# Pooled attention and a maxout feed-forward on one core: keys turned by the DMA crossbar, stores of whole tiles, one more half group, and first adds of batch 0's values on VectorE

## The chip, the cores and the metric

The kernel runs on one core of one Trainium2 chip. The metric is the device time in microseconds (us) of one execution. Before the change it is 242.86 us, the median of 3 runs (242.78 to 244.19). A core has five engines with queues of their own, which run in parallel and wait for each other by semaphores: TensorE (PE in the profile) for matmuls and transposes, VectorE (DVE), ScalarE (ACT), GpSimd (POOL), and SyncE (SP), which here only issues DMAs. Results of TensorE land in PSUM; DVE and ACT copy them to SBUF, the working memory. DMAs move data between SBUF and the memory in which inputs and outputs lie; a DMA can also transpose 16-bit data on its way through the crossbar.

## The reference, cut to what matters

There are 8 batches, 8 heads, 576 rows and 64 columns per head. Keys and values are averaged over groups of 8 rows, so that 72 pooled rows remain; each query attends to these. The attention output goes through three weight matrices of 512 x 768, of whose products the elementwise maximum is taken, and then through one of 768 x 512:

```python
k_p = k.reshape(B, H, Sp, pool, D).mean(axis=3)
v_p = v.reshape(B, H, Sp, pool, D).mean(axis=3)
scores = scale * np.matmul(q, k_p.transpose(0, 1, 3, 2))
...
x = np.ascontiguousarray(attn_out.transpose(0, 2, 1, 3)).reshape(B * S, H * D)
h = np.maximum(np.maximum(x @ w1, x @ w2), x @ w3)
return (h @ w_out)
```

## The kernel before

**Tokens and blocks.** The 4608 tokens are worked in 9 blocks of 512, numbered 0 to 8. Block n runs `hidden` (for each of 6 column groups jc of the hidden layer, three weight matrices, so 18 steps called slots) and then `project` (4 tiles of 128 tokens, one slot each). Attention of batch b = n + 1 is laid between the slots of block n, since a batch of 576 tokens is needed from block n + 1 on. Nothing is left to a scheduler: the order in which the code emits instructions is the order in which each engine runs them, and the plan (a table from slot to steps) says after which slot which step is emitted. Steps are named by a letter: `k` fills the key tile, `s` does the scores and exponentials of a head, `v` the attention values of 128 tokens, `x` their transposition into xT, `T` the transposition of the next batch's queries by DMA.

**Keys.** POOL folds the keys of batches 2 to 7 by adds into kps, twice side by side (`fold_k`, line 144, called from `pool_work`). `keys` (L171) turns kps on TensorE in six transposes into a PSUM tile pkt, and `fill_kz` (L177) copies it in two halves into kz, the layout that the scores need; batch 1 uses ACT for these copies and the others DVE (L187). Batch 0 is done ahead of block 0 by hand.

**Values of batch 0.** `pool_v` (L152) sums the 8 rows of each group on TensorE: 8 matmuls against an identity matrix, accumulating in PSUM, then a DVE copy to vp_all. It is called for heads 0 to 3, 4 to 5 and 6 to 7 (lines 418 to 421), in between the scores of the second half of the tokens (`scores2`). The other batches' values are folded on POOL.

**Start of block 0.** Block 0 begins when only the first 128 tokens are through attention. `hidden` therefore splits its work by columns of tokens (lines 315 and 316): group 0 for tokens 0 to 127 and 128 to 255, group 1 for tokens 0 to 255, then groups 0 and 1 for tokens 256 to 511, and the remaining groups in full width. `plan` of block 0 (lines 447 to 453) lays the rest of batch 0's attention and all of batch 1's between these slots.

**Stores.** A tile of 128 rows in osb holds two groups of 64 tokens: the tokens of a batch are kept in the order of their remainder g by 9, in the sequence GS. Row r of group g belongs to output row 9 r + GS[g]. Each group is stored by a DMA of its own (lines 337 to 341), 64 rows of 2 KB, issued by SP. The last tile is projected in two column halves, which ACT and DVE copy; there SP and ACT issue one group each. osb has 5 buffers, so a store has until the fifth next tile.

**SP's queue** holds, in order of emission, the query transposes, the xT transposes of batches 2 and later (`turn_x`, L220) and the stores. An entry that waits holds up those behind it.

Of the kernel before, what the change touches and what calls it, by code (L numbers as in the profile page):

```python
# [10 lines left out]
ALU = mybir.AluOpType  # L11
# [3 lines left out]
def kernel(  # L15
# [11 lines left out]
    nc = tc.nc  # L27
    dt = mybir.dt
    F32, BF16, F16 = dt.float32, dt.bfloat16, dt.float16

    B, H, S, D = q.shape
    POOL = 8
    Sp = S // POOL
# [8 lines left out]
    NG = 9  # L42
    GS = (0, 2, 4, 6, 8, 1, 3, 5, 7)
    NR = 64
    KCH = C // 128
    JCH = DFF // 128
    TOK = B * S
    NB = 512
    PSUM = bass.MemoryType.PSUM

    const = ctx.enter_context(tc.tile_pool(name="const", bufs=1))
    ld = ctx.enter_context(tc.tile_pool(name="ld", bufs=2))
    sb2 = ctx.enter_context(tc.tile_pool(name="sb2", bufs=2))
# [1 line left out]
    psp = ctx.enter_context(tc.tile_pool(name="psp", bufs=1, space=PSUM))  # L55
    ctx.enter_context(tc.manual_schedule())

    kts, vts, qbs, kps, qTs, ets = {}, {}, {}, {}, {}, {}

    def after(loads, first):  # L60
        for x in loads:
# [47 lines left out]
    identh = const.tile([128, 128], F16, name="identh", tag="identh")  # L109
    make_identity(nc, identh)  # L110
    for i in range(3):
# [6 lines left out]
        out=wo_sb, in_=moe_w_out.rearrange("(jc p) c -> p jc c", p=128))  # L118
# [22 lines left out]
    def new_kp(b):  # L141
        kps[b] = sb2.tile([96, 6, 2, D], BF16, name="kp", tag="kp")
# [9 lines left out]
    def pool_v(b, h, g, tag, evac):  # L152

        pvp = psp.tile([128, g - h, D], F32, name="pvp", tag=tag[0], bufs=tag[1])
        for j in range(POOL):
            nc.tensor.matmul(pvp, identh[0:Sp, :], vts[b][:, h:g, j, :],  # L156
                             start=(j == 0), stop=(j == POOL - 1))
        evac(out=vp_all[:, b, h:g, 0:D], in_=pvp[0:Sp])

    def turn_q(b, n0, n1, evac, tag):  # L160
# [10 lines left out]
    def keys(b, tag):  # L171
        pkt = psp.tile([128, 6, 96], BF16, name="pkt", tag=tag[0], bufs=tag[1])
        for i in range(6):
            nc.tensor.transpose(pkt[:, i, :], kps[b][:, i, :, :], ident[0:96, 0:96])  # L174
        return pkt

    def fill_kz(b, par, h0, h1, pkt, evac):  # L177
        rows = slice(64 * par, 64 * par + 64)
        evac(out=kz_all[b % 2][rows, par, h0:h1, 0:Sp].rearrange(  # L179
                 "p h (r i) -> p h r i", i=6),  # L180
             in_=pkt[rows, :, 12 * h0:12 * h1].rearrange("p i (h r) -> p h r i", r=12))

    def turn_k(b):
        pkt = keys(b, TR)
        for par in range(2):
            fill_kz(b, par, 0, H, pkt,
                    nc.scalar.copy if b == 1 else nc.vector.tensor_copy)  # L187

    def pool_k(b, tag):

# [61 lines left out]
    TR = ("tr", 1)  # L252
# [5 lines left out]
    def do(b, steps):  # L258

        for name in steps.split():
            i = int(name[1:] or 0)
            if name[0] in "qQ":
                turn_q(b, *QS[i], nc.vector.tensor_copy if name[0] == "Q"
                       else nc.scalar.copy, TR)
            elif name[0] == "T":
                qTs[b] = sb2.tile([128, 2 * NG, 128], BF16, name="qT", tag="qT")
                nc.sync.dma_start_transpose(  # L270
                    out=qTs[b], in_=qbs[b].rearrange("p hp t d -> p (hp t d)"))
            elif name[0] == "k":
                turn_k(b)
            elif name[0] == "K":
                pool_k(b, PW)
            elif name[0] == "a":
                nc.vector.tensor_tensor(out=k16, in0=kts[b][:, :, 0:4],
                                        in1=kts[b][:, :, 4:8], op=ALU.add)
            elif name[0] == "s":
                if i == 0:  # L280
                    new_et(b)
                scores(b, i)
            elif name[0] == "v":
                xns[b, i] = values(b, CHUNKS[i][0])
            else:
                turn_x(b, *CHUNKS[i], xns[b, i], TR,
                       nc.vector.tensor_copy if name[0] == "X" else nc.scalar.copy)
# [23 lines left out]
    def hidden(n, hT):  # L311

        parts = [(0, JCH, 0, NB)]
        if n == 0:
            parts = [(0, 1, 0, 128), (0, 1, 128, 256), (1, 2, 0, 256), (0, 2, 256, NB),
                     (2, JCH, 0, NB)]
        elif n == 1:
            parts = [(0, 1, 0, 256), (0, 1, 256, NB), (1, JCH, 0, NB)]
        for j0, j1, c0, c1 in parts:
            for jc in range(j0, j1):  # L320
                yield from hidden_part(n, jc, c0, c1, hT)

    def project(n, hT):
        for mm in range(4):
            m = 4 * n + mm
            last = m == TOK // 128 - 1
            osb = sb3.tile([128, C], F32, name="osb", tag="osb", bufs=5)
            for c in ((slice(0, C // 2), slice(C // 2, C)) if last else (slice(0, C),)):
                po = psp.tile([128, c.stop - c.start], F32, name="po", tag="pw", bufs=3)
                for jc in range(JCH):  # L330
                    nc.tensor.matmul(po, hT[:, jc, bass.ts(mm, 128)], wo_sb[:, jc, c],  # L331
                                     start=(jc == 0), stop=(jc == JCH - 1))
                if c.start:
                    nc.vector.tensor_copy(out=osb[:, c], in_=po)
                else:
                    nc.scalar.copy(out=osb[:, c], in_=po)  # L336
                for u in range(2):
                    b, g = divmod(2 * m + u, NG)
                    dst = out[S * b:S * b + S, :].rearrange("(r g) c -> r g c", g=NG)
                    (nc.scalar if last and u else nc.sync).dma_start(  # L340
                        out=dst[:, GS[g], c], in_=osb[64 * u:64 * u + 64, c])
            yield

    def new_hT():
# [8 lines left out]

    new_et(0)
    ATT = ("att", 2)
    new_kp(0)
    k16 = const.tile([96, 6, 4, D], F16, name="k16", tag="k16")
    heat(17)
    for i in range(0, 6, 2):
        src = kts[0][:, i:i + 2] if i else kt0  # L360
        f = const.tile([96, 2, 4, D], F32, name="kf", tag="kf")
        nc.vector.tensor_tensor(out=f, in0=src[:, :, 0:4], in1=src[:, :, 4:8],  # L362
                                op=ALU.add)
        nc.vector.tensor_tensor(out=f[:, :, 0:2], in0=f[:, :, 0:2], in1=f[:, :, 2:4],  # L364
                                op=ALU.add)
        nc.vector.tensor_tensor(  # L366
            out=kps[0][:, i:i + 2].rearrange("p i a d -> p a i d"),
            in0=f[:, None, :, 0].to_broadcast([96, 2, 2, D]),
            in1=f[:, None, :, 1].to_broadcast([96, 2, 2, D]), op=ALU.add)
    turn_q(0, 0, 5, nc.vector.tensor_copy, PW)  # L370
    turn_q(0, 5, 9, nc.scalar.copy, ATT)
    pkt0 = [keys(0, PW) for _ in range(2)]
# [4 lines left out]
    def scores4(h):  # L377
        psc = psp.tile([128, 4, 256], F32, name="psc4", tag="att", bufs=2)
        for i in range(4):
            score(0, h + i, psc[:, i, :], 0, 0, 4)  # L380
        exp(ets[0][:, h:h + 4, 0:256], psc[0:Sp])

    def scores2(h):
        psc = psp.tile([128, 2, 512], F32, name="psc2", tag="att", bufs=2)
        for i in range(2):
            score(0, h + i, psc[:, i, 0:64], 0, 4, 5)
            score(0, h + i, psc[:, i, 64:320], 1, 0, 4)
        exp(ets[0][:, h:h + 2, 256:S], psc[0:Sp, :, 0:320])
# [26 lines left out]
    turn_q(0, 14, 18, nc.vector.tensor_copy, PW)  # L415
    heat(2)
    scores4(4)
    pool_v(0, 0, 4, PW, nc.vector.tensor_copy)
    scores2(0)
    pool_v(0, 4, 6, PW, nc.vector.tensor_copy)  # L420
    pool_v(0, 6, 8, PW, nc.vector.tensor_copy)
    scores2(2)
# [9 lines left out]
    def block(n, plan):  # L432

        hT = new_hT()
        slot = 0
        for part in (hidden(n, hT), project(n, hT)):
            for _ in part:
                if slot == 0 and n > 0:
                    pool_work(n, mms[-1])
                for b, steps in plan.get(slot, ()):  # L440
                    if b < B:
                        do(b, steps)
                slot += 1

    fold_v(1)
    fold_k(2, nc.gpsimd)
    block(0, {0: [(0, "X1")], 3: [(0, "v2")], 5: [(0, "v3")], 6: [(0, "x2")],
              8: [(0, "x3")], 10: [(0, "v4")], 12: [(0, "x4")],
              13: [(1, "a")], 15: [(1, "K")], 17: [(1, "k")], 19: [(1, "Q0")],
              20: [(1, "Q1")], 21: [(1, "Q2 s0")], 22: [(1, "Q3 s1")],  # L450
              23: [(1, "s2 s3")], 24: [(1, "s4 s5")], 25: [(1, "s6 s7")],
              26: [(1, "v0")], 27: [(1, "v1 x0"), (2, "T")], 28: [(1, "v2 x1")],
              29: [(1, "v3 x2")], 30: [(1, "v4")]})


    def plan(n):
        b, i = n + 1, 3 * (n == 1)
        got = {0: [], 3: [], 3 + i: [(b, "k")]}
        got.update({5 + i + h: [(b, f"s{h}")] for h in range(H)})
        got[12 + i].append((b + 1, "T"))  # L460
        got.update({15 + i + c: [(b, f"v{c} x{c}")] for c in range(5)})
        if n == 1:
            got[0].append((1, "x3"))
            got[3].append((1, "x4"))
        return got
# [45 lines left out]
```

The softmax here doesn't subtract the row's maximum and nothing guards it: scores larger than these inputs give would overflow.

## Time and profile before

| what | value |
|---|---|
| device time, median of 3 | 242.86 us |
| profiled span, first to last instruction | 241.0 us |
| TensorE busy | 230.9 us (96%) |
| VectorE busy | 131.7 us (55%) |
| ScalarE busy | 100.1 us (42%) |
| GpSimd busy | 123.7 us (51%) |
| TensorE in the chain of work that ended last | 89% of the span |
| key transposes on TensorE (L174) | 54, 6 in a batch's turn |
| key copies on DVE, 64 x 576 | 12, mean 755 ns; on ACT 2, mean 633 ns |
| stores of half tiles, 128 KB | 70 on SP, 2.4 us to landing (median) |

TensorE is without a gap from about 41 us to 236 us; a steady block takes 24.3 us. Before that, it waits for inputs and for the first values to pass through the short chain of attention. Idle time of another engine costs nothing as long as TensorE doesn't wait for it. In the profile a row of a group of instructions gives line, engine, operation, output and input tiles with shapes, the count, and then the busy us and the mean ns of one.

### The profile page before, as it was taken

The page shows a single profiled execution, that of the slowest core. Times are in us where ns is not written, and L with a number is a line of the kernel's source. Part 1 is how long each engine was busy: PE and PEld are TensorE (multiplying, and loading weights), DVE is VectorE, ACT ScalarE, POOL GpSimd, SP SyncE. Part 2 cuts the span into 40 slices and gives each one's busy share as a digit, 9 for nine tenths or more (in the row PEclk, how much of TensorE's full clock was granted, in tenths as well). Part 3 has the DMA queues.
Part 4 walks back from the last instruction along what each step waited for, and adds up shares of the span by engine and source line. Part 5 has one row for each costly group of instructions (what it writes and reads, how often), then busy time and mean ns, then how long its engine had stood idle before and what let it go on. Part 6 is the DMA issues. An engine that isn't in the chain of part 4 may idle for free.

```text
span 241.0 us, 4221 instructions
## 1 busy us (share of the span) xinstructions
PE 230.9 (96%) x1609; PEld 122.7 (51%) x1609; DVE 131.7 (55%) x239; ACT 100.1 (42%) x173; POOL 123.7 (51%) x91
## 2 busy tenths in 40 slices
PE   7698999999999999999999999999999999999992
PEld 3376555575554555455545554555455544444441
DVE  6856754665583558354836483648364834504530
ACT  2373247546513651365235523552355232142121
POOL 8864276989997479638880979286500000000000
PEclk9999999999999999999999999999999999999999
DMA  7999999999948995699769987997640253043006
GB/s 135 188 198 206 196 202 208 169 166 241 184 97 153 222 166 120 128 194 197 131 125 156 227 176 133 193 192 135 133 93 0 69 123 85 3 108 66 0 20 154
DMA packets 51939, 34.29 MB, mean 142 GB/s; under 512 B 32144, under 2 KB 46480, under 8 KB 51920
## 3 DMA queue, kind: packets, MB, share of 16 engines
q0 software_dynamic: 17088, 17.11, 45.5%
q1 hardware_dynamic: 34672, 16.79, 34.3%
q8 instruction: 12, 0.20, 0.3%
q10 hardware_dynamic: 160, 0.13, 0.2%
q14 instruction: 7, 0.06, 0.1%
HBM read 34.60 MB, written 9.44 MB: 183 GB/s over the span
## 4 chain that ended last, share of the span: by engine, by line
PE 89%; DVE 5%; ACT 2%; DMA 2%; issue 1%; DVEq 0%
PE pw L295 55%; PE po L331 19%; PE psc L203 6%; PE pav L238 4%; DMA kt<-in_k_dram 2%; PE pxt L229 1%; DVE kf L362 1%; ACT et L208 1%; DVE t L304 1%; PE pkt L174 1%; PE pvp L156 1%; DVE xn L246 1%; PE pqt L167 1%; DVE kp L366 1%; DVE kf L364 1%
## 5 line engine op out<-in xcount | busy, mean ns | idle before, releaser
L295 PE MATMUL pw<-xT,mw 128*128 128x512 f16 (+2 forms) x696 | 155.6, 364 | 0.8 <-ACT xT L233 0.7
L295 PEld LDWEIGHTS <-mw 128*128 128x128 f16 x696 | 61.8, 98 | 56.2 <-issue 1.0
L304 DVE TENSOR_TENSOR t<-t,pw 128x512 f16<-128x512 f16 (+2 forms) x58 | 37.8, 651 | 71.0 <-PE pw L295 43.7
L301 ACT CAST t<-pw 128x512 f16<-128x512 f32 (+2 forms) x58 | 32.3, 556 | 56.1 <-PE pw L295 54.8
L331 PE MATMUL po<-mwo,hT 128*128 128x512 f16 (+1 forms) x222 | 50.7, 373 | 0.0
L208 ACT ACTIVATE et<-psc 72x576 f16<-72x576 f32 (+2 forms) x62 | 40.7, 662 | 20.9 <-PE psc L203 20.7
L307 DVE TENSOR_TENSOR hT<-t,pw 128x512 f16<-128x512 f16 (+2 forms) x58 | 37.7, 650 | 9.0 <-PE pw L295 5.3
L336 ACT COPY osb<-po 128x512 f32<-128x512 f32 (+1 forms) x36 | 20.9, 580 | 47.7 <-PE po L331 43.7
L135 POOL TENSOR_TENSOR half<-vt 72x2048 f32<-72x2048 f16 x7 | 28.4, 4060 | 10.0 <-DMA vt<-in_v_dram 9.9
L331 PEld LDWEIGHTS <-hT 128*128 128x128 f16 x222 | 20.3, 97 | 21.3 <-DVE hT L307 2.4
L135 POOL TENSOR_TENSOR half<-kt 96x1536 f32<-96x1536 f16 x6 | 18.5, 3085 | 23.4 <-DMA kt<-in_k_dram 23.3
L246 DVE TENSOR_TENSOR xn<-pav,rcp 128x512 f16<-128x512 f32 x39 | 27.0, 691 | 1.5 <-DVE rcp L244 0.2
L136 POOL TENSOR_TENSOR half<-half 72x1024 f32<-72x1024 f32 (+1 forms) x13 | 27.2, 2096 | 1.0
L203 PE MATMUL psc<-qT,kz 128*128 128x64 bf16 (+3 forms) x192 | 25.9, 246 | 0.4 <-DVE kz L179 0.3
L203 PEld LDWEIGHTS <-kz 128*128 128x128 bf16 x192 | 17.8, 98 | 15.7 <-DVE kz L179 1.5
L238 PEld LDWEIGHTS <-et 72*128 72x128 f16 x312 | 15.2, 98 | 7.6
L238 PE MATMUL pav<-vp,et 72*128 72x65 f16 x312 | 16.5, 194 | 0.0
L244 DVE RECIPROCAL rcp<-pav 128x8 f32<-128x8 f32 x39 | 7.9, 204 | 9.4 <-PE pav L238 9.3
L139 POOL TENSOR_TENSOR kp<-half 96x384 bf16<-96x384 f32 x12 | 11.7, 993 | 0.5
L179 DVE COPY kz<-pkt 64x576 bf16<-64x576 bf16 (+1 forms) x14 | 9.9, 711 | 2.9 <-PE pkt L174 2.7
L79 POOL DMA_DIRECT2D vt<-in_v_dram x10 | 8.0, 804 | 2.9 <-DMA qb<-in_q_dram 2.2
L139 POOL TENSOR_TENSOR vp<-half 72x512 f16<-72x512 f32 x7 | 8.9, 1268 | 0.5
(48 smaller groups left out, 79.1 us busy)
## 6 DMA issues: line engine op xcount, KB each, us to landing
out_dram<-osb SPq DMA_DIRECT2D x70, 128.0 KB, 2.4
kt<-in_k_dram POOLq DMA_DIRECT2D x7, 576.0 KB, 7.4
qb<-in_q_dram POOLq DMA_DIRECT2D x7, 576.0 KB, 12.2
vt<-in_v_dram POOLq DMA_DIRECT2D x7, 576.0 KB, 15.0
mw<-in_moe_w_dram POOLq DMA_DIRECT2D x9, 256.0 KB, 9.3
mwo<-in_moe_w_out_dram POOLq DMA_DIRECT2D x1, 768.0 KB, 18.1
qb<-in_q_dram POOLq DMA_DIRECT2D x2, 288.0 KB, 7.0
xT<-xn SPq DMA_TRANSPOSE x30, 2.4
```

The lines of the kernel that those rows point to most:

```text
L135: e.tensor_tensor(out=f, in0=t[:, :, 0:4, :], in1=t[:, :, 4:8, :], op=ALU.add)
L136: e.tensor_tensor(out=f[:, :, 0:2, :], in0=f[:, :, 0:2, :], in1=f[:, :, 2:4, :], op=ALU.add)
L203: nc.tensor.matmul(out, kz_all[b % 2][:, f % 2, h, :], qTs[b][:, n + i0:n + i1, 64 * (h % 2):64 * (h % 2) + 64], start=True, stop=True)
L208: nc.scalar.activation(out=out, in_=in_, func=FT.Exp, scale=1.0 / 64.0)
L238: nc.tensor.matmul(pav[:, h // 4, 65 * (h % 4):65 * (h % 4) + 65], ets[b][:, h, c0:c0 + 128], vp_all[:, b, h, :], start=True, stop=True)
L246: nc.vector.tensor_tensor(out=xn, in0=pv[:, :, :, 0:D], in1=rcp.to_broadcast([128, 2, 4, D]), op=ALU.mult)
L295: mm = nc.tensor.matmul(pw, w_sb[wi][:, kc, bass.ts(jc, 128)], xT[:, kc, col], start=(kc == 0), stop=(kc == KCH - 1))
L301: nc.scalar.copy(out=t, in_=pw)
L304: nc.vector.tensor_tensor(out=t1, in0=t, in1=pw, op=ALU.max)
L307: nc.vector.tensor_tensor(out=hT[:, jc, c0:c1], in0=t, in1=pw, op=ALU.max)
L331: nc.tensor.matmul(po, hT[:, jc, bass.ts(mm, 128)], wo_sb[:, jc, c], start=(jc == 0), stop=(jc == JCH - 1))
L336: nc.scalar.copy(out=osb[:, c], in_=po)
```

## The change

It has four parts.

- **Keys by the crossbar.** For batches 3 to 7 a new step `Z`, emitted in the block before the keys are needed (slot 17), issues a DMA transpose of kps into an SBUF tile kT on SP. `turn_k` copies from kT in place of pkt; the copies of all batches but 2 are on ACT.
- **Whole-tile stores.** Where both groups of a tile are of one batch and stand in rising order, one DMA stores all 128 rows. Its source is 128 partitions, its destination a view of 2 x 64 rows of 512. In the last tile, ACT issues the first column half and SP the second.
- **One more early half group.** In block 0, hidden group 2 too is split by tokens, 0 to 255 first. Block 0 has three more slots, and its plan is laid out anew.
- **First adds of batch 0's values.** DVE adds rows 0 to 3 and 4 to 7 of each group, and TensorE then sums 4 rows in place of 8; the scores of heads 0 and 1 are emitted ahead of the first of these sums.

The key step of later blocks moves from slot 3 to 2, and the values from slots 15 to 19 to slots 14 to 18. The diff, cut to its core:

```diff
     def pool_v(b, h, g, tag, evac):
-        for j in range(POOL):
-            nc.tensor.matmul(pvp, identh[0:Sp, :], vts[b][:, h:g, j, :],
-                             start=(j == 0), stop=(j == POOL - 1))
+        nc.vector.tensor_tensor(out=v16[:, h:g], in0=vts[b][:, h:g, 0:4],
+                                in1=vts[b][:, h:g, 4:8], op=ALU.add)
+        for j in range(4):
+            nc.tensor.matmul(pvp, identh[0:Sp, :], v16[:, h:g, j, :],
+                             start=(j == 0), stop=(j == 3))
...
     def turn_k(b):
-        pkt = keys(b, TR)
+        pkt = keys(b, TR) if b < 3 else kTs[b]
         for par in range(2):
             fill_kz(b, par, 0, H, pkt,
-                    nc.scalar.copy if b == 1 else nc.vector.tensor_copy)
+                    nc.vector.tensor_copy if b == 2 else nc.scalar.copy)
...
+            elif name[0] == "Z":
+                kTs[b] = sb2.tile([128, 6, 96], BF16, name="kT", tag="kT")
+                nc.sync.dma_start_transpose(
+                    out=kTs[b], in_=kps[b].rearrange("p i a d -> p (i a d)"))
...
-            parts = [(0, 1, 0, 128), (0, 1, 128, 256), (1, 2, 0, 256), (0, 2, 256, NB),
-                     (2, JCH, 0, NB)]
+            parts = [(0, 1, 0, 128), (0, 1, 128, 256), (1, 3, 0, 256), (0, 3, 256, NB),
+                     (3, JCH, 0, NB)]
...
+                e = nc.scalar if last and c.start == 0 else nc.sync
+                b, g = divmod(2 * m, NG)
+                dst = out[S * b:S * b + S, :].rearrange("(r g) c -> g r c", g=NG)
+                if g < NG - 1 and GS[g] < GS[g + 1]:
+                    step = GS[g + 1] - GS[g]
+                    e.dma_start(out=dst[GS[g]:GS[g + 1] + 1:step, :, c],
+                                in_=osb[:, c])
+                    continue
                 for u in range(2):
                     b, g = divmod(2 * m + u, NG)
-                    dst = out[S * b:S * b + S, :].rearrange("(r g) c -> r g c", g=NG)
-                    (nc.scalar if last and u else nc.sync).dma_start(
-                        out=dst[:, GS[g], c], in_=osb[64 * u:64 * u + 64, c])
+                    dst = out[S * b:S * b + S, :].rearrange("(r g) c -> g r c", g=NG)
+                    e.dma_start(out=dst[GS[g], :, c], in_=osb[64 * u:64 * u + 64, c])
...
     scores4(4)
+    scores2(0)
     pool_v(0, 0, 4, PW, nc.vector.tensor_copy)
-    scores2(0)
...
-        got = {0: [], 3: [], 3 + i: [(b, "k")]}
+        got = {0: [], 3: [], (3 + i if n == 1 else 2): [(b, "k")]}
...
-        got.update({15 + i + c: [(b, f"v{c} x{c}")] for c in range(5)})
+        got.update({14 + i + c: [(b, f"v{c} x{c}")] for c in range(5)})
+        got[17 + i].append((b + 1, "Z"))
```

## The prediction

> **What bounds the kernel now.** I read the stage table first (one row per block of 512 tokens: busy us of each engine, granted clock, DMA share, GB/s), then the chain of work that ended last, the DMA view of a stretch in which only stores run, and the timeline of the tail. Lines of the stage table, for blocks 1, 3, 5, 6 and the last:
>
> ```profile
> 49.00:73.40 24.40, 24.40 (x185) 13.81 (x184) 14.99 (x28) 11.28 (x21) 23.16 (x13) 1.00 0.92 176
> 97.70:122.00 24.30, 24.30 (x167) 12.49 (x166) 13.81 (x24) 10.73 (x18) 15.63 (x10) 1.00 0.96 166
> 146.40:170.70 24.30, 24.30 (x168) 12.51 (x167) 13.90 (x24) 10.73 (x18) 16.53 (x11) 1.00 0.95 163
> 170.70:195.00 24.30, 24.30 (x168) 12.54 (x167) 13.89 (x24) 10.73 (x18) 1.65 (x2) 1.00 0.34 75
> 215.80:241.00 25.20, 20.73 (x102) 9.76 (x100) 8.68 (x13) 6.23 (x11) 0.00 (x0) 0.98 0.29 66
> ```
>
> The second number is PE: it fills every block, at full clock. So from 41 us to 236 us only PE's work sets the time, and what leaves PE is won one for one. But the next-to-last column is the one to keep in mind: in blocks 1 to 5 each of the 16 DMA engines is busy 0.88 to 0.96 of the time. DMA has almost no room there if its work is spread unevenly. In the first stages the same column reaches 1.37 (9 to 17 us), so packets of one engine can overlap somewhat.
>
> Pieces of the chain (start, us, what): the sums of batch 0's values, and the keys of one batch turned by PE:
>
> ```profile
> 12.82 0.88 PE pvp L156 x8
> 13.69 0.28 PE psc L203 x4
> 13.97 0.89 PE pvp L156 x16
> ...
> 29.97 0.27 PE pkt L174 x6
> ```
>
> A stretch with stores alone (212 to 233 us; packets, MB, share of 16 engines), and the issues with their time to landing:
>
> ```profile
> q1 hardware_dynamic: 640, 1.05, 22.9%
> ...
> out_dram<-osb SPq DMA_DIRECT2D x8, 128.0 KB, 2.3
> ```
>
> 640 packets for 8 stores are 80 each: 64 rows of 2 KB and 16 completion writes, so each half-tile store ran on all 16 DMA engines. 22.9% of 16 x 21 us is 77 engine-us, over 512 rows 0.15 us for a row. The tail (start, us, engine, line):
>
> ```profile
> 233.27 5.17 SPq L340 DMA_DIRECT2D out_dram<-osb  x8
> 236.31 1.22 ACTq L340 DMA_DIRECT2D out_dram<-osb  x2
> 236.56 0.42 DVE L334 COPY osb<-po 128x256 f32<-128x256 f32 x1 [4.51 <-PE po L331]
> ```
>
> The last tiles leave PE 1.3 us apart, the last result stands at 236.98 us, and the span ends at 241.0.
>
> **What the Trainium skill says.** (1) "DMA: Bandwidth & Descriptors", section "Why a DMA increments its semaphore by 16 and not by 1": a copy runs on the largest k up to 16 that divides the slowest non-size-1 dimension of both access patterns; such a copy from SP or ACT takes the lowest-numbered k engines, and only those post completions. The 16 completion writes per store above agree for 64 rows against 64 partitions; no DMA of the kernel before has a short slowest dimension, so the trace doesn't show the other side. (2) Same page, "Queues, rings and completion order": one sequencer's DMAs stand in one ring per engine, begun in order, and an engine alternates between rings by packet; not shown by this trace. (3) Same page, "Issuing engines are not separate DMA queues": SP's and ACT's DMAs share the same 16 engines, so a second queue saves issue time alone.
>
> **The change part by part.**
>
> *Whole-tile stores.* The build shows what the diff doesn't say outright: of 36 tiles 28 (all whose first group g isn't 4 or 8) are now stored by one DMA whose source is 128 partitions, but whose destination is 2 x 64 rows of 512, the 2 slowest. By (1) the largest k that divides 128 and 2 is 2: engines 0 and 1 alone. The price of a row is bounded by 0.15 us above (in 64-partition stores) and by the page's specification of about 27 GiB/s per engine below (2 KB: 0.07 us, an estimate); the trace's packet records have 0.087 us for a store's first rows, before its engines meet, and I take that. A whole tile is 64 rows per engine: 64 x 0.087 = 5.6 us, where a half now takes 4 rows of 0.15 = 0.6 us.
>
> Tail: tiles 32 to 35 are all whole; the last in two column halves (ACT the first, SP the second, by (3) on the same two engines). 3 x 5.6 + 128 rows of 1 KB at about half = 5.6: 22.4 us, from the first issue at 233.3 plus 0.6: data end near 256.3, against about 240 now. About +17 us, hidden by nothing.
>
> Pace of blocks 1 to 5: each engine is now busy 0.92 x 24.4 + (0.88 + 0.96 + 0.95) x 24.3 + 0.94 x 24.4 = 113 us of 121.7. The half stores in it are 8 x 64 x 0.15 / 16 = 4.8 us per block, 24 in all; 89 remain for loads and transposes. Engines 0 and 1 get in their place the stores of blocks 0 to 4, which stand in SP's ring ahead of block 5's transposes: 16 whole ones x 5.6 = 90, four split ones x 1.2 = 5, and some 4 for the new key transposes: 188 us for 121.7. If packet times exclude each other, that is +66 us; if they overlap as at the densest stage (1.37), 188 / 1.37 = 137, +15 us. I take the middle, +40. PE feels it because transposed queries and attention rows stand behind stores in SP's ring, and loads need all engines; five osb buffers let stores lag by about one block.
>
> *Keys by the crossbar* (batches 3 to 7). Removes 6 transposes of 0.27 us on PE per batch: 5 x 0.27 = -1.35 us. Key copies go from DVE (2 x 0.755) to ACT (2 x 0.633, the row of the same shape), which waits 2 us at a time for PE between its casts in those slots: nothing. The new transpose waits on SP for POOL's folded keys; behind it stand the last xT transpose and the block's stores, and osb copies wait for those only a block later. POOL has the latest such keys done at 139.05 us, before SP is through that block's first xT transposes (140.26 + 3.83), and they are needed from 149 on: nothing by itself.
>
> *First adds of batch 0.* PE sums drop from 24 matmuls to 12: at most -0.9 us. But DVE's order is add, copy, add, copy, add, copy. From the 1536-wide f16 add of keys (0.948 us) I estimate 0.68 and twice 0.42 for 1024 and 512; copies are 0.425 and twice 0.29. Adds 1.52, copies 1.0, matmuls 0.45 + 2 x 0.22, some 0.3 for hand-overs: 3.7 us from about 12.6, so the last copy ends near 16.3, against 15.19 now. Scores 2, 3 and the first values stand behind those sums on PE: +1.0 us (0 if the wait hides behind the exponentials, +1.2 at most).
>
> *One more early half group.* 12 matmuls of 512 become 24 of 256: PE 3 x (2 x 0.44 - 0.86) = +0.06; ACT and DVE a few tenths, both with idle. PE idles 11.0 - 9.57 = 1.43 us between 17 and 28 us, waiting for xT; half a group (1.3 us) put in front of those waits can fill some: 0 to -1.0, I take -0.7.
>
> Sum: 242.86 - 1.35 + 1.0 - 0.7 = 241.8 without stores; with them + 17 + 40 = 299.
>
> **The rivals.** *A: the 2 x 64 destination is still spread over 16 engines.* For it: the rule is the page's, and no transfer here tests it for a short dimension. Then whole stores halve SP's issues (0.59 us each); the tail's last SP issue begins at 237.9 though its data stand at 236.98, so up to -0.9, I take -0.7: 241.8 - 0.7 = 241.1, between 239.3 and 242.5 by the start's and the group's bounds. This is the side where it isn't slower. *B: two engines, but the blocks hide it:* packets overlap better than anywhere in this trace and the one-block lag of osb takes the rest; only the tail pays: 241.8 + 17 = 259, 254 to 268. Against it: shares of 0.9 leave no room for 18 us more per block on two engines. *C: the key transpose is late* and SP stands still: a few us at most on A, since a score needs it eight us after it is issued.
>
> **How the numbers follow.** Two engines with pace and tail 0.46 (270 to 325, likeliest 299); B 0.14; A with C 0.40: a page's rule that no run here has tested for this shape gets no more than 0.6. A's values straddle the 1% bound at 240.4: 0.19 faster, 0.21 same; the rest is slower, 0.60. The range takes in A down to 239.3 and goes to 315, leaving the worst of the pace out.
>
> **What would show it.** Right: whole stores with 2 completion writes in place of 16 and 5 us or more to landing (2.4 now); PE waiting in blocks 1 to 5 for xT, qT or kz; a long tail of DMA after the last PE instruction at a small DMA share. Also: pkt of PE 24 matmuls, not 54; the last copy of values on DVE after 16 us; PE idle under 1.4 us between 17 and 28 us. Wrong: landings near 2.4 us with PE full in all blocks would mean rule (1) doesn't hold for this shape, and A stands.

## The result, and the profile after

The changed kernel takes 321.72 us (median of 4 runs, 320.19 to 323.05) against 242.82: a ratio of 1.323, with a 95% interval of 1.315 to 1.332. It is slower by 79 us. The forecast had the direction and the cause, whole-tile stores on two DMA engines, but with 299 us it was 23 us short, and the time lies above its range (239.3 to 315.0). Where a kernel below also had runs in a slower state (over 1.5% above its fastest run), the time given is the median of all its runs and the ratio that of the fast ones alone; leaving the slower ones out changes the median by no more than 0.4 us, but for the stores on ScalarE, whose time is given without them.

Stages of the changed kernel (window; us, then busy us and count of PE, PEld, DVE, ACT, POOL; granted clock of PE, DMA share, GB/s):

```profile
17.00:28.00 11.00, 10.93 (x127) 9.60 (x125) 7.47 (x22) 5.39 (x12) 4.38 (x6) 0.76 1.26 205
...
83.50:120.30 36.80, 25.89 (x161) 12.69 (x162) 12.14 (x22) 13.04 (x20) 16.66 (x10) 0.87 0.78 114
...
189.20:238.80 49.60, 34.10 (x188) 15.72 (x189) 13.54 (x25) 16.59 (x25) 20.28 (x13) 0.82 0.84 100
...
257.50:278.20 20.70, 20.70 (x98) 9.40 (x96) 8.24 (x12) 5.85 (x10) 0.00 (x0) 1.00 0.17 56
278.20:299.40 21.20, 20.79 (x103) 9.77 (x100) 8.62 (x13) 6.22 (x11) 0.00 (x0) 1.00 0.18 51
299.40:320.40 21.00, 0.00 (x0) 0.00 (x0) 0.05 (x1) 0.00 (x0) 0.00 (x0) 0.57 0.12 47
```

Three things stand in it. A loaded block (83.5 to 120.3) takes 37 us where it took 24.3, and PE works in 26 of them. The late blocks, which load nothing, run at their old pace. And behind the last result there are 21 us in which no engine works and the DMA share is 0.12: 2 of 16 engines, busy all the time, is 0.125.

The DMA view of the changed kernel's tail alone (302 to 318 us) says the same by count:

```profile
DMA packets 504, 0.80 MB, mean 50 GB/s; under 512 B 8, under 2 KB 214, under 8 KB 504
## 3 DMA queue, kind: packets, MB, share of 16 engines
q1 hardware_dynamic: 374, 0.67, 10.9%
q10 hardware_dynamic: 130, 0.13, 2.3%
```

50 GB/s on two engines is 25 GB/s each, 0.082 us for a row of 2 KB, in line with the 0.087 that the prediction took. Queue q10 holds ScalarE's one store of 128 rows: 130 packets, so 2 completion writes, where its two half stores before made 160 packets, 16 completion writes each. The 8 small packets of the window are then the completion writes of four stores. And since stores of SP (q1) and of ScalarE (q10) run in this window together and still only two engines are busy, they share the same two.

The queue of SP in the changed kernel (start, us, what; lines of two blocks) shows how blocks 1 to 5 feel it:

```profile
65.77 12.51 SPq L272 DMA_TRANSPOSE qT<-qb  x1
78.37 5.19 SPq L225 DMA_TRANSPOSE xT<-xn  x4
...
101.02 13.98 SPq L272 DMA_TRANSPOSE qT<-qb  x1
115.09 5.15 SPq L225 DMA_TRANSPOSE xT<-xn  x4
```

The query transpose, which SP issued in 3.4 to 4.6 us before, now takes 12.5 and 14.0 us to issue. The likely reason is that the rings of the two engines are full of rows to store; the trace doesn't show how full a ring is. The xT transposes come after it. The chain that ended last, at the first of these block ends, then reads:

```profile
76.34 1.31 PE po L337 x6
77.66 0.62 SPq L272
...
78.37 1.21 SPq L225
...
79.68 1.27 SPq L225
...
81.04 2.38 DMA xT<-xn
...
83.55 6.59 PE pw L301 x22
```

Read it from the bottom: the block's first matmuls waited for xT to land, xT for its place in SP's queue, and that for the query transpose. In the table of waits TensorE has 39.8 us for xT at four such places, where it had none:

```profile
PE pw L301 <- DMA xT<-xn: 39.8, 4, 14.3
...
PE psc L205 <- DMA qT<-qb: 2.3, 1, 2.3
```

Loads suffer with them: keys land 15.1 us after their issue (7.4 before), and POOL waits 46.3 us for them (23.3 before).

The tail of the changed kernel (start, us, engine, line):

```profile
295.73 8.51 SPq L348 DMA_DIRECT2D out_dram<-osb  x4
...
298.77 1.12 ACTq L348 DMA_DIRECT2D out_dram<-osb  x1
299.02 0.42 DVE L340 COPY osb<-po 128x256 f32<-128x256 f32 x1 [4.51 <-PE po L337]
```

The account of the 79.4 us of span: from the last result to the end 21.0 us in place of 4.0 (+17.0); PE idle before that 299.4 - 244.3 = 55.1 in place of 237.0 - 230.9 = 6.1 (+49.0); PE busy 244.3 in place of 230.9 (+13.4, with 30 matmuls fewer; the granted clock in the loaded blocks is 0.82 to 0.93, where it was 1.00).

### The profile page after: what moved, and what is told of

Same layout as the page of the kernel before. It is cut to its first block, busy times and chain, and to the rows that moved or that the text cites. A ratio compares the mean times of both kernels' runs of the same rounds, so it can differ in the third digit from the quotient of the medians.

```text
span 320.4 us, 4149 instructions
## 1 busy us (share of the span) xinstructions
PE 244.3 (76%) x1579; PEld 126.7 (40%) x1579; DVE 124.2 (39%) x233; ACT 112.3 (35%) x185; POOL 123.3 (38%) x91
## 2 busy tenths in 40 slices
DMA packets 54109, 35.02 MB, mean 109 GB/s; under 512 B 34314, under 2 KB 48650, under 8 KB 54090
## 4 chain that ended last, share of the span: by engine, by line
PE 64%; SPq 12%; DMA 10%; issue 3%; DVE 2%; ACT 1%; POOL 1%; DVEq 0%; POOLq 0%
PE pw L301 42%; PE po L337 13%; SPq L272 8%; PE psc L205 5%; SPq L225 4%; DMA qT<-qb 4%; DMA xT<-xn 3%; DMA vt<-in_v_dram 3%; PE pav L240 3%; ACT kz L181 1%; DMA kT<-kp 1%; PE pvp L158 1%; PE pqt L169 0%; POOL qb L86 0%; DVE t L310 0%
## 5 line engine op out<-in xcount | busy, mean ns | idle before, releaser
L301 PE MATMUL pw<-xT,mw 128*128 128x512 f16 (+2 forms) x708 | 167.7, 382 | 45.3 <-DMA xT<-xn 39.8
L301 PEld LDWEIGHTS <-mw 128*128 128x128 f16 x708 | 65.9, 103 | 108.3 <-issue 61.8
L337 PE MATMUL po<-mwo,hT 128*128 128x512 f16 (+1 forms) x222 | 49.8, 373 | 0.1
L210 ACT ACTIVATE et<-psc 72x576 f16<-72x576 f32 (+2 forms) x62 | 40.7, 662 | 24.3 <-PE psc L205 24.3
L135 POOL TENSOR_TENSOR half<-vt 72x2048 f32<-72x2048 f16 x7 | 28.4, 4053 | 24.3 <-DMA vt<-in_v_dram 24.3
L135 POOL TENSOR_TENSOR half<-kt 96x1536 f32<-96x1536 f16 x6 | 18.5, 3085 | 46.4 <-DMA kt<-in_k_dram 46.3
L205 PE MATMUL psc<-qT,kz 128*128 128x64 bf16 (+3 forms) x192 | 27.1, 254 | 3.4 <-DMA qT<-qb 2.3
L205 PEld LDWEIGHTS <-kz 128*128 128x128 bf16 x192 | 18.6, 102 | 20.0 <-DVE hT L313 2.6
L181 ACT COPY kz<-kT 64x576 bf16<-64x576 bf16 x10 | 11.6, 1162 | 6.8 <-DMA kT<-kp 6.6
L72 POOL DMA_DIRECT2D kt<-in_k_dram x9 | 5.1, 564 | 18.3 <-PE pw L301 13.5
## 6 DMA issues: line engine op xcount, KB each, us to landing
kt<-in_k_dram POOLq DMA_DIRECT2D x7, 576.0 KB, 15.1
```

What stands on the lines that cost most here:

```text
L135: e.tensor_tensor(out=f, in0=t[:, :, 0:4, :], in1=t[:, :, 4:8, :], op=ALU.add)
L205: nc.tensor.matmul(out, kz_all[b % 2][:, f % 2, h, :], qTs[b][:, n + i0:n + i1, 64 * (h % 2):64 * (h % 2) + 64], start=True, stop=True)
L210: nc.scalar.activation(out=out, in_=in_, func=FT.Exp, scale=1.0 / 64.0)
L301: mm = nc.tensor.matmul(pw, w_sb[wi][:, kc, bass.ts(jc, 128)], xT[:, kc, col], start=(kc == 0), stop=(kc == KCH - 1))
```

## The experiments

**Stores put back.** The changed kernel with the old store loop:

```diff
-                if g < NG - 1 and GS[g] < GS[g + 1]:
...
-                    e.dma_start(out=dst[GS[g]:GS[g + 1] + 1:step, :, c],
-                                in_=osb[:, c])
-                    continue
                 for u in range(2):
...
```

> The changed kernel with its stores put back to two DMAs of 64 rows per tile, all other parts kept. Theory (whole-tile stores run on two DMA engines and everything slow comes from that): 240 to 243 us, landing of stores near 2.4 us, no wait of TensorE in the blocks. Rival (the new key transposes hold up SP's queue, the stores only suffer from it): still above 290 us.

Measured: 243.52 us, ratio to before 1.003 (1.000 to 1.006). A block of it beside 24.3 us of before:

```profile
97.70:122.00 24.30, 24.15 (x162) 12.26 (x160) 12.11 (x22) 13.01 (x21) 16.72 (x11) 1.00 0.96 172
```

So the stores make 78 of the 79 us, and the other three parts together give nothing. The changed kernel and this one move the same 35.02 MB: it is the spread over engines that differs, not the amount.

**Whole-tile stores alone**, in the kernel before:

> The kernel before with whole-tile stores as its only change. Theory: 318 to 326 us, as slow as all four parts together, since the other three are worth a few us. Rival (the key transposes of the crossbar need SP's queue and share the blame): under 290 us.

Measured: 314.94 us, ratio 1.295 (1.287 to 1.302). The stores need no partner. The remaining 6.8 us came with the other parts; beside half stores these parts cost 0.7. Which of them weighs more beside full rings wasn't tried.

**The same bytes in one DMA per tile, over more engines.** The destination's shape differs, and all 36 tiles are stored in this way, not 28:

```diff
...
-                    e.dma_start(out=dst[GS[g]:GS[g + 1] + 1:step, :, c], in_=osb[:, c])
+                dst = out.rearrange("(a b) c -> a b c", a=16)[:, 8 * m:8 * m + 8, c]
+                e.dma_start(out=dst, in_=osb[:, c])
```

> The changed kernel, each tile still stored by one DMA of 128 rows, but into 16 pieces of 8 rows, so that the slowest dimension of the destination is 16 (rows land elsewhere in the output than the reference has them). Theory: 16 engines take part, 240 to 243 us. Rival (one DMA of 256 KB, or its scattered rows, is what costs): near 320 us.

Measured: 242.90 us, ratio 0.999 (0.997 to 1.001). One DMA of 256 KB in place of two costs nothing, and gains nothing, when the slowest dimension is 16. ScalarE's one store makes 144 packets here, so 16 completion writes.

With 4 pieces of 32 rows:

> The same with 4 pieces of 32 rows per tile (rows land elsewhere in the output). Theory: 4 engines, so 32 rows of 2 KB per engine and tile, 2.7 us. All 36 tiles, not 28. Tail about 11 us of stores in place of 22 (+7 us over the kernel before); engines 0 to 3 have 89 + 4 + 20 x 2.7 = 147 us of work in the 122 us of blocks 1 to 5, so 260 to 285 us in all. Rival (a fixed cost of any destination with a short slowest dimension): near 320 us.

Measured: 283.67 us, ratio 1.168 (1.160 to 1.176). Between 2 and 16, as the rule on the number of engines has it. ScalarE's one store makes 132 packets, so 4 completion writes, and the DMA share in the tail is 0.25, 4 of 16 engines. The span ends 11.3 us after the last result at 269.7 (21.0 with two engines, 4.0 before), and the same query transposes take 9.4 and 8.8 us to issue:

```profile
64.13 9.35 SPq L272 DMA_TRANSPOSE qT<-qb  x1
...
95.33 8.84 SPq L272 DMA_TRANSPOSE qT<-qb  x1
```

**Tail and pace apart.** Whole-tile stores in the last block only, and everywhere but there (`n == 8` or `n < 8` added to the condition):

> The changed kernel with whole-tile stores in the last block alone (tiles 32 to 35), two half stores in all others. Only the tail can pay: 22 us of stores on two engines after the last results, so 16 to 18 us over the changed kernel with half stores everywhere (243.5 us): 259 to 262 us. If the tail's cost were mostly carried over from stores of earlier blocks: under 255 us.

> The changed kernel with whole-tile stores everywhere but in the last block. The pace of the blocks alone: 321.7 - 17 = 305 us. If tail and pace don't add up: off by more than 4 us.

Measured: 259.9 us (ratio 1.070, 1.067 to 1.073) and 303.92 us (1.253, 1.251 to 1.255). Against half stores (243.5) the tail is +16.4 and the pace +60.4, and both together make 320.3: they add up to the changed kernel's 321.7 but for 1.4 us.

**Which engines, and which ring.** Whole-tile stores issued by GpSimd (`nc.gpsimd.dma_start` in place of `e.dma_start`):

> The changed kernel with its whole-tile stores issued by GpSimd in place of SP and ScalarE. Still two engines for each store, but, if the Trainium skill is right, another pair each time. Theory (engines 0 and 1 are overfull because every store lands on the same two): the blocks run at full pace again and only the tail pays, some 5 us for one store on one pair: 245 to 255 us. Rival (a store on two engines is slow to land, and osb or the queue waits for it, whichever engines they are): above 290 us.

Measured: 292.78 us, ratio 1.203 (1.196 to 1.209). The theory is refuted, and the time lies just above the rival's bound. In its tail the DMA share is 0.42 and 0.50 (windows 278 to 282 and 282 to 286 us), 7 to 8 engines: the stores don't all run on one pair, in line with the Trainium skill ("DMA: Bandwidth & Descriptors", section "Why a DMA increments its semaphore by 16 and not by 1": from GpSimd, k consecutive engines from a round-robin cursor; that they are consecutive this trace doesn't show). The DMA view has the rest (kind, engine, count, KB, us to landing; then packets, MB and share of 16 engines between 278 and 290 us):

```profile
out_dram<-osb POOLq DMA_DIRECT2D x27, 256.0 KB, 11.5
kt<-in_k_dram POOLq DMA_DIRECT2D x7, 576.0 KB, 15.5
...
qT<-qb SPq DMA_TRANSPOSE x6, 4.3
...
q0 software_dynamic: 1652, 1.01, 34.4%
```

Transposes on SP land fast again, but a store takes 11.5 us, and the key load issued behind the stores on GpSimd takes 15.5; the chain that ended last now runs through these loads (15.5, 14.4, 15.8 and 17.6 us) and POOL's folds. So the hold-up moved to the loads, and the rival had it in kind: a store that is slow to land holds up what stands behind it in the queue, though no pair gets all the stores. Of the 50 us of span over the kernel before, 9 are in the tail and 41 before it. The run changes more than the pair, however: 1.01 MB in 34.4% of 16 x 12 us is 15 GB/s per busy engine, where SP's stores had about 24 (0.80 MB in 13.2% of 16 x 16 us), and GpSimd has the loads and folds to do as well. So it doesn't tell how stores on changing pairs would do from SP.

Whole-tile stores issued by ScalarE (`nc.scalar.dma_start`):

> The changed kernel with its whole-tile stores issued by ScalarE: the same two engines and the same bytes on each, but a ring of their own, so that SP's transposes no longer stand behind them. Theory A (the transposes' place behind the stores in SP's ring is what TensorE waits for): under 290 us. Theory B (engines 0 and 1 have more to move than the blocks last, whatever the order): 305 us or more; ScalarE, held up while its ring is full, can make it slower still.

Measured: 331.6 us, the mean of 330.49 and 332.74, ratio 1.365 (1.357 to 1.373); two further executions took 348 us. With the stores off SP's queue its query transposes take less time to issue in blocks 1 to 5 (2.4 to 8.5 us in four, 10.5 in one, against 7.4 to 15.1), but ScalarE stands still at its own issues, up to 12.2 us at a time, and TensorE waits for it: 18.9 us for casts and 18.3 us for key copies. This speaks against order alone as the cause; it doesn't prove the other, since ScalarE's hold-up comes on top.

**Fewer loads beside the stores.**

```diff
-            after([load_k(n + 2)], mm)
-            load_q(n + 2)
-            load_v(n + 2)
+            kts[n + 2], qbs[n + 2], vts[n + 2] = kts[2], qbs[2], vts[2]
```

> The changed kernel without the loads of batches 3 to 7, which work on batch 2's keys, queries and values instead (so the output of those batches isn't the reference's). Theory B: each engine loses some 11 us of load packets per block, 54 us in all, so engines 0 and 1 have 134 us in place of 188 in 122 us of blocks: 265 to 280 us, of which 17 are the tail. Theory A: SP's ring holds the same stores and transposes in the same order, so nearly no change, over 305 us.

Measured: 278.01 us, ratio 1.144 (1.140 to 1.148). With 16.4 us for the tail, the pace is down from +60 to about +18 (278.0 - 16.4 - 243.5), although SP's ring holds the same entries in the same order, and its query transposes still take as long:

```profile
56.02 12.74 SPq L272 DMA_TRANSPOSE qT<-qb  x1
83.98 13.25 SPq L272 DMA_TRANSPOSE qT<-qb  x1
```

TensorE waits 9.3 us for xT in place of 39.8. So some 42 of the 60 us need the loads beside the stores; the order of SP's queue and its long issues, without them, make no more than the 18 that are left. How the loads add their part this run doesn't separate: by their packets on the two engines, or by landing late themselves (keys 15.1 us after their issue, 7.4 before).

**The clock.** Dummy matmuls ahead of blocks 2 to 6:

```diff
+        if 2 <= n <= 6:
+            wm2 = psp.tile([128, 512], F32, name="wm2", tag="tr", bufs=1)
+            for _ in range(24):
+                nc.tensor.matmul(wm2, warm[:, 0:128], warm, start=True, stop=True)
```

> The changed kernel with 24 dummy matmuls of 512 columns ahead of the first matmul of blocks 2 to 6 (5.2 us at full clock), where TensorE stands still for 5 us or more. Theory A (the halved clock after each stall is a cost of its own): 4 to 8 us less than the changed kernel. Theory B (engines 0 and 1 set the pace, and a faster TensorE only waits longer): within 2 us of 321.7.

Measured: 321.11 us, ratio 1.324 (1.319 to 1.329). From 49 us to the end of the loaded blocks (about 240 us) the granted clock rises from 0.88 to 0.93, and the time stays. So this part of the lower clock is a consequence of the stalls and costs nothing of its own.

**The other three parts, each alone in the kernel before.**

> The kernel before with the first adds of batch 0's values on VectorE, and its scores ahead of their sums, as its only change. The prediction had +1.0 us for the longer hand-over chain. New theory: TensorE also waits long enough in that chain for its granted clock to be halved for some us, so +2 to +3 us (245 to 246 us), with a clock under 1.00 in the stage from 9 to 28 us. Rival (the wait hides behind the exponentials): within 0.5 us of before.

Measured: 245.00 us, ratio 1.009 (1.006 to 1.012): +2.1 us. TensorE in this kernel (start, us, tiles, and what ended the idle time before):

```profile
13.26 0.60 PE L158 MATMUL pvp<-v,identh 72*128 72x256 f16 x4
14.71 0.40 PE L158 MATMUL pvp<-v,identh 72*128 72x128 f16 x4 [0.85 <-DVE v L155]
15.82 0.40 PE L158 MATMUL pvp<-v,identh 72*128 72x128 f16 x4 [0.71 <-DVE v L155]
16.05 0.44 PE L205 MATMUL psc<-qT,kz 128*128 128x64 bf16 x4
16.33 0.51 PE L400 MATMUL pav<-vp,et 72*128 72x65 f16 x8
```

It waits twice for VectorE, and the scores and first values stand behind; the first values begin at 16.3 us where they began at 15.0. In the next stage (17 to 28 us) the granted clock is 0.86, where it was 1.00. That this makes the rest of the 2.1 us is likely; no run takes it apart.

> The kernel before with the keys of batches 3 to 7 turned by the crossbar, and the plan of the later blocks that goes with it, as its only change. Theory: 5 x 0.27 = 1.35 us less, 241.5 us. Rival (SP's queue or the copies on ScalarE hold TensorE up): no gain.

Measured: 243.59 us, ratio 1.001 (0.997 to 1.004). The gain of 1.35 us isn't seen. The profiled run took 241.83 and has TensorE without new waits; others of the same kernel took up to 244.53, and where they lose time no profile shows. This stays open.

> The kernel before with one more half group in block 0, and block 0's plan, as its only change. Theory: TensorE's idle time between 17 and 28 us is partly filled, 0 to -1.0 us, most likely -0.7 (242.1 us).

Measured: 243.62 us, ratio 1.002 (0.998 to 1.005): no gain. PE is busy 10.52 us of the 11 in the stage from 17 to 28 us (9.57 before), so the idle time was filled, and yet the kernel isn't faster. In the profiled run TensorE waits 1.5 us for batch 2's transposed queries, which it didn't before; whether this is the loss in all runs isn't shown.

> The changed kernel without its whole-tile stores and without the first adds on VectorE: keys by the crossbar and one more half group alone. Theory: the two gains add up to about -2.0 us, 240.8 us, faster than the kernel before and the changed one. Rival (they fill the same idle time or get in each other's way): not better than the better of the two.

Measured: 242.28 us, ratio 0.995 (0.992 to 0.998), about -1.2 us: the one version that beats both kernels, if barely. It keeps the half stores and the sums on TensorE.

## Why the prediction was wrong

1. *Two engines.* Right: 2 completion writes and 0.12 of the DMA engines in the tail. The rule of the Trainium skill ("DMA: Bandwidth & Descriptors", section "Why a DMA increments its semaphore by 16 and not by 1") is shown by this case for a destination of 2, 4 and 16 pieces: 130, 132 and 144 packets for a store of 128 rows. The prediction gave this case 0.46 and the spread over 16 engines 0.40, so it was no firm forecast. One of its signs, the landing of whole stores after 5 us or more, can't be read: the trace has no landing time for them.
2. *Tail.* Right: +17 forecast, +16.4 alone and +17.0 in the profile.
3. *Pace: the step that failed.* The prediction had two ends, +66 if packets of one engine exclude each other and +15 if they overlap as at the densest stage, and took "the middle, +40". Measured +60.4. The 1.37 of the densest stage came from loads alone; it gave no ground to believe that stores make room for loads. With 2 engines the exclusive sum of +66 is 6 us above what was measured. With 4 engines the exclusive sum (147 us of work in 122) has +25, and the run took +33 (283.7 - 243.5 - 7.3 of tail, where the tail's 7.3 is 11.3 - 4.0); without later loads it has +12 (134 in 122), and the run took +18. All three lie within 8 us of the exclusive sum. That the sum on the two engines is what sets the pace fits these runs and isn't proven by them: from GpSimd, where no pair had all the stores, some 40 us were lost as well. The term was mis-sized by 20 us, nearly the whole miss of 23.
4. *How PE feels it.* Right in kind: xT and query transposes behind the stores, and late loads. What the prediction left out is that SP itself stands at the issue, up to 15 us. Of order against amount, the run with fewer loads gives the amount of work beside the stores the greater weight; ScalarE's and GpSimd's runs moved the order and brought hold-ups of their own, so they leave this open.
5. *First adds.* Forecast +1.0, measured +2.1 (1.4 to 2.8). The chain was right: the last copy was forecast to end near 16.3 us and ended at 16.5, and the first values began 1.3 us later. What wasn't counted is the fall of the clock after the waits, the likely rest.
6. *Keys and half group.* Forecast -1.35 and -0.7, measured +0.1 (-0.7 to +1.0) and +0.4 (-0.4 to +1.1) alone, and -1.2 (-2.0 to -0.5) together. The sum without stores was forecast at 241.8 and measured at 243.5. "Nothing" for the key copies on ScalarE was priced with the wrong row: from kT they take 1.162 us, not 0.633; whether this costs time no run shows.
7. *Rival A* (spread over 16 engines, 241.1) is refuted for this shape; given 16 pieces it is what the kernel does, at 242.9. *Rival B* (tail only, 259) is what whole stores in the last block alone cost (259.9), but the blocks hid nothing of the rest, +60.4. *Rival C* (the key transpose is late) has no sign in the keys alone, +0.1.

## What to carry over

Read a DMA's shape as the engines see it: one short slowest dimension (here the 2 of the destination's 2 x 64) can put a transfer on that many of 16 engines, while bytes, count and mean DMA share look the same or better. When a few engines get the work of all, add up that engine's packets against the stage and take the plain sum, which here came within 8 us in three runs; a share over 1 in some other stage is no proof of room. Then look at both ends of the loss, the tail and the loads and transposes in between, and measure them apart.

## What the runs showed of the hardware

- The time to issue a DMA differed with what else was in flight: the same transpose took SP 3.4 to 4.6 us to issue in the kernel before (2.6 to 5.4 with the stores put back), and 7.4 to 15.1 us with stores on two engines.
- ScalarE copies 64 x 576 16-bit values in 0.632 us from PSUM and 1.162 us from SBUF, with the same shape on both sides. Two groups of the changed kernel:

```profile
L181 ACT COPY kz<-kT 64x576 bf16<-64x576 bf16 x10 | 11.6, 1162 | 6.8 <-DMA kT<-kp 6.6
...
L181 ACT COPY kz<-pkt 64x576 bf16<-64x576 bf16 x2 | 1.3, 632 | 0.3 <-PE pkt L176 0.2
```

- Waits of 0.7 and 0.85 us of TensorE in the start, with 2.0 us idle in the 8 us of that stage (0.3 before), were followed by a granted clock of 0.86 between 17 and 28 us in the first adds alone. It is 0.91 with the stores put back and 0.76 with all parts, and 1.00 in the profiles of the keys alone, the half group alone and both together, which leave the adds out.
